# Two weight loads of a fused attention and GLU kernel issued from ScalarE's DMA queue

## The chip, the cores and the metric

The kernel runs on one core of a Trainium2 chip. The metric is the device time of one execution in microseconds (us); lower is better. All runs named here were fast, with a granted TensorE clock of 1.00 (0.999 in a few, 0.996 in one). The profile is of one execution, and its span is about 1.3 us shorter than the time of the same execution (557.7 against 558.93 for the kernel before).

## The reference, cut to what matters

```python
# x: (1, 2048, 576) bf16
xn = layernorm(x)
s  = attention(xn, wqkv, wo)          # 32 heads of 18, causal window of 256
g  = silu((sigmoid(xn @ w_gate) * (xn @ w_up)) @ w_down)   # w_gate, w_up: 576 x 4608
out = x + s * g
```

The first 512 rows of x are loaded and normalized, and then the gate/up products begin.

## The kernel before

The program is a graph of operations that a small scheduler puts into one list for each engine. The parts that matter:

```python
NWARM = (43, 10)      # warming products, two matmuls each
...
def load_x(self, c, i=0):             # the first four x tiles: four loads on SyncE
    if c == 0:
        for i in range(BPC):
            self.x_dma[i] = (self.dma(self.x0[:, i, :], self.x[i * P:(i + 1) * P, :], ...
...
zero = self.hT[:, 0, 0:P]
z = op("DVE", 920, lambda e: e.memset(zero, 0.0), "init:zero", prio=0)
...
self.op_tab = op("ACT", 1500, lambda e: e.activation(self.tring[:, 0, 0:1], zero[:, 0:1], ACTF.Exp), "init:tab",
                 deps=[z], prio=0)    # ScalarE's table load stands before it (0.79 to 2.07 us)
self.warm(NWARM[0], z, None, 107)     # TensorE multiplies zeros until x is there
...
def weights(wg):                      # one group: 256 columns of w_gate and of w_up, 256 KB each
    ds = [self.load_nat(self.wgs[:, sw, :, i, :], w[:, fc], f"dma:w:{c}:{wg}", ("w", sw, i), pr, [dw])
          for i, w in enumerate((self.wg, self.wu))]
    if wg % 2 == 0:                   # remainders: 64 rows for two groups, 64 KB each
        self.op_wgr[wg] = self.load_rem(self.wgr[:, sr, :], (self.wg[:, f8], self.wu[:, f8]), ...
...
def pair(eng, outs, lhs, rhs, start, stop, swap=0):   # every product: two matmuls on two row halves
    for i in range(2):
        t = i ^ swap
        res = eng.matmul(outs[i], lhs(ROWS[t], i), rhs(ROWS[t], i), start=start, stop=stop, tile_position=(64 * t, 0))
```

For each matmul TensorE has two instructions in its program, a weight load and the product (8342 of each in the profile); "instruction pair" below means these two. SyncE issues, in this order: four x tiles, the first group (gate, up), its two remainders, the second group, the second remainders, and so on.

The softmax here doesn't subtract the row's maximum and nothing guards it: scores larger than these inputs give would overflow.

Of the kernel before, what the change touches and what calls it, by code (L numbers as in the profile page):

```python
# [249 lines left out]
class Builder:  # L250
# [834 lines left out]
    def schedule(self):  # L1085
        ENGS = ("PE", "ACT", "DVE", "POOL", "SP")
        ops = self.ops
        remaining = [len(o.deps) + len(o.odeps) for o in ops]
        ready_t = [0.0] * len(ops)
        enabled = {e: [] for e in ENGS}  # L1090
        for i, o in enumerate(ops):
            assert o.cidx == i
            if remaining[i] == 0:
                enabled[o.eng].append(o)
        free = {e: 0.0 for e in ENGS}
        bw_clock = 0.0
        prog = {e: [] for e in ENGS}
        nsched = 0
        last_sc = 0.0
        while nsched < len(ops):  # L1100
            best = None
            for e in ENGS:
                cand = enabled[e]
                if not cand:
                    continue
                claims = {}
                if e == "PE":
                    for o in cand:
                        if o.acq is not None:
                            due = last_sc + o.space if o.space else 0.0  # L1110
                            claims.setdefault(o.acq.pool.name, []).append((o.prio, o.cidx, max(ready_t[o.cidx], due)))
                bk = None
                for o in cand:
                    st = max(free[e], ready_t[o.cidx])
                    early = 0.0
                    if o.space:
                        early = min(max(0.0, last_sc + o.space - st), FILL_NS)
                    units = None
                    if o.acq is not None:
                        mine = o.acq.pool  # L1120
                        barred = set()
                        for other in (self.pool_s, self.pool_f):
                            if other is not mine and any((p_, c_) < (o.prio, o.cidx) and r_ <= st + SHARE_NS
                                                         for p_, c_, r_ in claims.get(other.name, ())):
                                barred |= set(other.units)
                        got = mine.pick(o.acq.n, st, barred)
                        if got is None:
                            continue
                        st = max(st, got[0])
                        units = got[1]  # L1130
                        if any((p_, c_) < (o.prio, o.cidx) and r_ <= st + 300.0 for p_, c_, r_ in claims[mine.name]):
                            continue
                    k = (st + early + o.prio * self.PRIO_NS, o.cidx)
                    if bk is None or k < bk[0]:
                        bk = (k, o, st, units)
                if bk is not None and (best is None or (bk[2], ENGS.index(e)) < best[0]):
                    best = ((bk[2], ENGS.index(e)), bk)
            if best is None:
                left = [o.name for o in ops if o.idx < 0][:20]
                raise RuntimeError(f"scheduler stuck; unresolved ops e.g. {left}")  # L1140
            _, o, stt, units = best[1]
            if o.space:
                last_sc = stt
            if o.eng == "PE":
                if o.name.startswith("f1"):
                    for d in [d for d in ops if d.filler is not None and d.idx < 0]:
                        d.filler.rel.remove(d)
                        d.idx = nsched
                        nsched += 1
                        if d in enabled["PE"]:  # L1150
                            enabled["PE"].remove(d)
            enabled[o.eng].remove(o)
            if o.acq is not None:
                o.deps += [d for d in o.acq.pool.take(o.acq, units) if d not in o.deps]
            o.start = stt
            if o.lane is not None:
                free[o.eng] = stt + o.est
                o.end = max(stt + o.est + DMA_LAT_NS, bw_clock + o.nbytes / DMA_BYTES_PER_NS + DMA_QUEUE_NS)
                o.end += o.slack
                bw_clock = max(bw_clock, stt + o.est) + o.nbytes / DMA_BYTES_PER_NS  # L1160
            else:
                o.end = stt + o.est
                free[o.eng] = o.end
            o.idx = nsched
            nsched += 1
            prog[o.eng].append(o)
            for s_ in o.succs:
                remaining[s_.cidx] -= 1
                if s_.eng == o.eng:
                    lat = TURN_WAIT_NS if o.eng == "PE" and o in s_.deps else 0.0  # L1170
                elif o.lane is not None:
                    lat = DMA_PE_NS if s_.eng == "PE" else 90.0
                else:
                    lat = PE_OUT_NS if o.eng == "PE" else PE_IN_NS if s_.eng == "PE" else 50.0
                ready_t[s_.cidx] = max(ready_t[s_.cidx], o.end + lat)
                if remaining[s_.cidx] == 0 and s_.idx < 0:
                    enabled[s_.eng].append(s_)
        self.prog = prog
        if self.verbose:
            for e in ENGS:  # L1180
                busy = sum(o.est for o in prog[e] if o.filler is None)
                print(f"[sched] {e}: n={len(prog[e])} busy={busy / 1e3:.1f}us end={max(o.end for o in prog[e]) / 1e3:.1f}us")
# [97 lines left out]
```

## Time and profile before

| | before |
|---|---|
| median of 3 runs | 559.06 us (559.03 to 559.08) |
| span in the profile | 557.7 us |
| TensorE busy | 552.4 us (99%) |
| first gate/up product | 7.74 us |
| first x tile landed | 3.01 us |

The prediction shows the main lines. Two more turn out to matter, from the list of DMA queues on the page of the kernel before (packets, megabytes, share of the 16 DMA engines' time):

```profile
q1 hardware_dynamic: 105960, 60.68, 39.7%
...
q8 instruction: 66, 1.08, 0.8%
```

q1 is SyncE's queue. q8 brings instructions in 66 packets of 16 KB. TensorE's program has 8342 pairs and 221 other recorded instructions, 16,905 in all; 66 x 16,384 bytes over 16,905 is about 64 bytes for each, so this looks like TensorE's program streaming in, 256 instructions a packet. (The figure is rough: a part of the program was there before the first packet, which starts at 7.89 us, with TensorE at work from 1.05. The stops below give the 256 exactly.)

### The profile page before, as it was taken

What the parts mean: (1) busy time and instruction counts of PE and PEld (TensorE: products, weight loads), DVE (VectorE), ACT (ScalarE), POOL (GpSimd) and SP (SyncE); (2) the same over time, 40 slices, a digit from 0 to 9 for tenths busy, and PEclk for the clock granted to TensorE, in tenths of its full rate; (3) what the DMA queues carried; (4) which work ended last, traced back from release to release, by engine and by line L of the source; (5) the groups of instructions that cost most, each with busy time, mean ns of one, the idle gap of its engine ahead of it and who ended that gap; (6) DMA issues with size and microseconds to landing.
All of it is one profiled execution on the core that took longest, in us unless ns stands there. A gap on an engine that the chain in (4) does not pass through costs nothing.

```text
span 557.7 us, 19262 instructions
## 1 busy us (share of the span) xinstructions
PE 552.4 (99%) x8342; PEld 339.1 (61%) x8342; DVE 333.6 (60%) x797; ACT 274.3 (49%) x383; POOL 210.3 (38%) x360
## 2 busy tenths in 40 slices
PE   8999999999999999999999999999999999999997
PEld 7454444677755545457886555645588754444787
DVE  5477788787568667674558757357567623333133
ACT  4245654443656655645656464565756433223011
POOL 5564456566245454440667434034382200000000
PEclk9999999999999999999999999999999999999999
DMA  7988997831125535534121264234511035552010
GB/s 217 323 234 190 223 264 211 213 58 45 53 73 155 159 108 145 142 108 96 29 63 44 72 192 123 82 117 140 171 31 38 24 115 148 169 151 68 2 45 24
DMA packets 113468, 67.83 MB, mean 122 GB/s; under 512 B 18620, under 2 KB 111516, under 8 KB 113384
## 3 DMA queue, kind: packets, MB, share of 16 engines
q1 hardware_dynamic: 105960, 60.68, 39.7%
q0 software_dynamic: 7424, 5.92, 4.0%
q8 instruction: 66, 1.08, 0.8%
q14 instruction: 18, 0.15, 0.1%
HBM read 55.15 MB, written 2.36 MB: 103 GB/s over the span
## 4 chain that ended last, share of the span: by engine, by line
PE 98%; DVE 1%; DMA 0%; issue 0%; DVEq 0%
PE ps L122 95%; PE ps L801 3%; DMA x<-in_A_x_dram 0%; DVE small L525 0%; DVE small L527 0%; DVE xnr L541 0%; PE ps L599 0%; DVE s_attn L1062 0%; DVE thf L1067 0%; DVE xnr L545 0%; DVE small L529 0%; DVE small L531 0%; DVE xf L1072 0%; DVEq L1227 0%
## 5 line engine op out<-in xcount | busy, mean ns | idle before, releaser
L122 PE MATMUL ps<-xnT,wgs 64*128 64x512 bf16 (+1 forms) x2400 | 282.6, 368 | 0.2
L751 ACT ACTIVATE expr<-ps 128x1024 bf16<-128x1024 f32 (+4 forms) x160 | 154.9, 969 | 77.8 <-PE ps L122 77.2
L122 PEld LDWEIGHTS ps<-xnT,wgs 64*128 64x128 bf16 x2400 | 113.9, 94 | 115.0 <-DVE hT L949 1.6
L122 PE MATMUL ps<-wd_sb,hT 64*128 64x288 bf16 (+2 forms) x2448 | 156.7, 276 | 0.0
L949 DVE SCALAR_TENSOR_TENSOR hT<-tring,ps 128x512 bf16<-128x512 bf16 x144 | 98.3, 683 | 94.7 <-ACT tring L946 93.6
L946 ACT ACTIVATE tring<-ps 128x512 bf16<-128x512 f32 x144 | 86.1, 598 | 129.6 <-PE ps L122 127.5
L122 PEld LDWEIGHTS ps<-wd_sb,hT 64*128 64x128 bf16 x2448 | 112.5, 94 | 28.5
L279 POOL DMA_DIRECT2D qk<-qd x160 | 82.2, 521 | 119.9 <-PE ps L122 109.6
L764 DVE TENSOR_TENSOR expr<-expr,mask 128x128 bf16<-128x128 bf16 (+2 forms) x240 | 63.6, 299 | 62.3 <-ACT expr L751 61.7
L715 POOL TENSOR_SCALAR kx<-kprev,small 128x256 bf16<-128x256 bf16 x64 | 61.3, 967 | 28.2 <-PE ps L122 27.4
L122 PE MATMUL ps<-qk,kx 64*128 64x320 bf16 (+1 forms) x704 | 59.4, 254 | 0.0
L279 POOL DMA_DIRECT2D oT<-o2T x72 | 36.4, 513 | 58.7 <-DVE o2T L827 49.8
L122 PE MATMUL ps<-xnT,wgr 64*128 64x512 bf16 (+1 forms) x300 | 56.0, 367 | 0.0
L122 PEld LDWEIGHTS ps<-qk,kx 64*128 64x128 bf16 x704 | 31.2, 94 | 21.5 <-ACT expr L751 0.6
L122 PE MATMUL ps<-xnT,wqk 64*128 64x512 bf16 x256 | 32.6, 376 | 0.0
L1052 ACT ACTIVATE thf<-ps 128x576 bf16<-128x576 f32 (+3 forms) x22 | 11.4, 519 | 39.7 <-PE ps L122 39.4
L819 DVE STREAM_TRANSPOSE ot<-ps 128x512 f32<-128x512 f32 x32 | 22.4, 700 | 11.6 <-PE ps L801 11.5
L715 DVE TENSOR_SCALAR kx<-qk,small 128x512 bf16<-128x512 bf16 x64 | 22.4, 378 | 4.7 <-PE ps L122 4.1
L122 PEld LDWEIGHTS ps<-xnT,wgr 64*128 64x128 bf16 x300 | 14.9, 94 | 16.5
L827 DVE STREAM_TRANSPOSE o2T<-o 128x512 bf16<-128x512 bf16 x32 | 22.7, 711 | 1.0
L637 DVE CAST qd<-ps 128x1024 bf16<-128x1024 f32 (+1 forms) x20 | 22.1, 1111 | 1.5 <-PE ps L122 1.5
L697 ACT ACTIVATE v_aug<-ps 64x288 bf16<-64x288 f32 x32 | 13.1, 409 | 17.3 <-PE ps L122 16.8
(71 smaller groups left out, 300.9 us busy)
## 6 DMA issues: line engine op xcount, KB each, us to landing
wgs<-in_B_w_gate_dram SPq DMA_DIRECT2D x72, 256.0 KB, 3.3
wgs<-in_B_w_up_dram SPq DMA_DIRECT2D x72, 256.0 KB, 3.9
wd_sb<-in_B_w_down_dram SPq DMA_DIRECT2D x9, 576.0 KB, 6.3
qk<-qd POOLq DMA_DIRECT2D x100, 36.0 KB, 2.6
wgr<-in_B_w_gate_dram SPq DMA_DIRECT2D x36, 64.0 KB, 2.3
wgr<-in_B_w_up_dram SPq DMA_DIRECT2D x36, 64.0 KB, 2.7
xf<-in_A_x_dram SPq DMA_DIRECT2D x16, 144.0 KB, 2.6
out_dram<-xf SPq DMA_DIRECT2D x15, 144.0 KB, 1.8
```

The costliest lines, as they stand in the source:

```text
L122: res = eng.matmul(outs[i], lhs(ROWS[t], i), rhs(ROWS[t], i), start=start, stop=stop, tile_position=(64 * t, 0))
L279: o = self.op(eng, DMA_ISSUE_NS[eng], lambda e: e.dma_start(dst, src), name, deps, prio, nbytes=nbytes)
L637: return eng.tensor_copy(dst, self.both(h, n))
L697: return eng.activation(dst, src, ACTF.Copy)
L715: return e.tensor_scalar(self.kx[:, sx, pos:pos + n_ // SW, t, :], src.rearrange("p (s k) -> p s k", k=SW), self.half[:, t:t + 1], None, A ...
L751: return eng.activation(self.expr[:, se, :, lo * SW:NT], self.both(h, NT)[:, :, lo * SW:NT], ACTF.Exp, scale=SM_SCALE)
L764: return eng.tensor_tensor(e_, e_, m_, ALU.mult)
L801: res = eng.matmul(outs[i][p0:p0 + VH, cols], self.v_aug[ROWS[i], o:o + VH], self.expr[ROWS[i], se, t, cols], start=n == 0, stop=n == len( ...
L819: return e.transpose(self.ot1[:, p1, :], self.halves(hp, NT)[i])
L827: t2 = op("DVE", dve_ns(NT), lambda e, p2=p2, p3=p3: e.transpose(self.o2T[:, p3, :], self.o2[:, p2, :]), f"ot2:{c}:{pr}:{i}", deps=[on, d3 ...
L946: th = op("ACT", act_ns(NT), lambda e: e.activation(self.tring[:, st, :], bank(h, 0), ACTF.Tanh, scale=0.5), f"th:{c}:{ft}", deps=[pg, dt_ ...
L949: mu = op("DVE", dve_ns(NT), lambda e: e.scalar_tensor_tensor(self.hT[:, ft, :], self.tring[:, st, :], 1.0, bank(h, 1), ALU.add, ALU.mult) ...
```

## The change

The intent: start the first weight loads while SyncE is still busy with x, on a queue that is idle then, and let SyncE go on 1 us sooner with what follows. ScalarE issues the two loads right after the dummy activation (2.09 to 2.30 us in the trace of the kernel before) that follows its table load (0.79 to 2.07).

```diff
@@ at the end of the scheduler
+        first = [o for o in prog["SP"] if o.name == "dma:w:0:0"]
+        for o in first:
+            prog["SP"].remove(o)
+            o.eng = "ACT"
+            o.deps.append(self.op_tab)
+        at = prog["ACT"].index(self.op_tab) + 1
+        prog["ACT"][at:at] = first
         self.prog = prog
```

Nothing else in the five programs changes.

## The prediction

> **What bounds the kernel now.** I read the page's busy shares first, then a table of engine busy time by stretch, then the chain of waits, and last the timeline of the first ten microseconds. The shares and the table say where there is anything to win:
>
> ```profile
> PE 552.4 (99%) x8342; PEld 339.1 (61%) x8342; DVE 333.6 (60%) x797; ACT 274.3 (49%) x383; POOL 210.3 (38%) x360
> ...
> 0.00:7.70 7.70, 5.68 (x126) 5.22 (x126) 4.38 (x17) 3.74 (x8) 2.97 (x12) 1.00 0.72 197
> 7.70:12.20 4.50, 4.46 (x156) 4.24 (x158) 2.10 (x15) 1.39 (x2) 2.82 (x4) 1.00 0.87 249
> 12.20:554.60 542.40, 542.25 (x8068) 329.61 (x8061) 325.88 (x762) 268.68 (x372) 204.47 (x345) 1.00 0.44 120
> ```
>
> The first figure after the comma is TensorE's busy time. From 12.2 to 554.6 us TensorE is idle 0.15 us (542.40 less 542.25). The whole body is TensorE's own work at full clock, so a load that comes earlier there is worth nothing. A change in the loading order can act only through the moment at which TensorE starts its first real product; from then on, a shift of that moment is a shift of the end. The chain of waits shows that moment:
>
> ```profile
> 0.80 2.21 DMA x<-in_A_x_dram
> ...
> 6.66 0.41 DVE xnr L541
> 7.06 0.02 issue
> 7.09 0.19 DVE xnr L545
> 7.28 0.04 issue
> 7.32 0.32 PE ps L599 x10
> 7.64 0.10 issue
> 7.74 1.00 PE ps L122 x26
> ```
>
> The first x tile lands at 3.01 us. VectorE does the layer norm of two tiles until 7.28, TensorE transposes the second tile (L599) from 7.32, and the gate/up stream (L122) begins at 7.74. The reader is to distrust the "0.10 issue" before it: that is time for which the profile found no wait. The timeline of what is concerned shows more:
>
> ```profile
> 2.09 0.21 ACT L452 ACTIVATE tring<-hT 128x1 bf16<-128x1 bf16 x1
> ...
> 2.66 0.43 SPq L279 DMA_DIRECT2D wgs<-in_B_w_gate_dram  x1
> 3.14 0.51 SPq L279 DMA_DIRECT2D wgs<-in_B_w_up_dram  x1
> 3.69 0.55 SPq L279 DMA_DIRECT2D wgr<-in_B_w_gate_dram  x1
> 4.28 0.59 SPq L279 DMA_DIRECT2D wgr<-in_B_w_up_dram  x1
> ...
> 4.48 0.68 ACT L586 ACTIVATE tring<-x 128x576 bf16<-128x576 bf16 x1 [2.19 <-DMA x<-in_A_x_dram]
> ...
> 7.71 0.80 PEld L122 LDWEIGHTS ps<-xnT,wgs 64*128 64x128 bf16 x24 [0.19 <-issue]
> ```
>
> By the list of DMA issues in a narrow window, the gate load of 2.66 lands 4.1 us later (6.76) and the up load of 3.14 lands 4.5 us later (7.64). The first weight load of the stream is at 7.71, 0.07 us after that. So two paths end almost together: the norm of the second tile, and the landing of the up weights; the landing is the later one. Without it the stream would follow the transposes as it does later in the same timeline, where transposes at 8.56 and 10.03 are followed by products at 8.71 and 10.17, 0.14 to 0.15 us later. That would be 7.32 + 0.15 = 7.47, so the landing holds TensorE for 7.74 - 7.47 = 0.27 us.
>
> The trace also has the landing of each of the 16 increments of a load. Those of the up load come at 6.06 to 6.54 for thirteen of them, and at 6.91, 7.37 and 7.60 for three: the wait is for the slowest of the 16 DMA engines.
>
> [...]
>
> **The change part by part.** (1) *Removed from SyncE:* two issues, 2.66 to 3.69, so 1.03 us. The small gate/up remainders (wgr) are issued at about 2.66 in place of 3.69, and everything behind them up to 1.03 us earlier. Worth nothing directly: TensorE waits for none of it (the remainder's last share is in at 8.16, first used at 8.45 by the weight loads).
>
> (2) *Added to ScalarE:* two issues after the dummy activation that ends at 2.09 + 0.21 = 2.30. At SyncE's 0.43 and 0.51 us they occupy 2.35 to about 3.35. ScalarE's next work is at 4.48 and waits for the third x tile, so about 1.1 us of its 2.19 us idle time is left. Cost 0[...].
>
> (3) *Moved in time:* the gate issue from 2.66 to 2.35, the up issue from 3.14 to about 2.85: 0.3 us earlier each. SyncE's first load is issued at 0.80 and its first packet moves at 1.84, so 1.04 us: the gate data can flow from 3.4.
>
> (4) *Moved in order:* before, one row serves x, then the gate and up weights, then the remainders, then the second group. x packets (1152 B) run from 1.84 to 4.53, weight packets (512 B) from 3.96. After, the weights have a row to themselves[...]. At 3.4 about 350 KB of x had moved and 226 KB were left, 14 KB per engine; the first group is 512 KB, 32 KB per engine. [...] Two live rows may also move more than one: with 64 and 144 KB loads beside each other at 14 to 16 us the core moved 348 GB/s, against 256 to 280 at 2 to 4 us. [...] The stragglers' lag of about a microsecond comes on top in both cases. [...] I put the landing 0.2 to 0.9 later than 7.64, mid 0.5.
>
> (5) *x tiles delayed by the sharing:* the fourth lands at about 4.84, used at 5.85, and may come 0.3 to 0.6 later: hidden. The third (4.46) may come 0.1 to 0.3 later; its statistics feed the norm at 7.49 and the transposes at 8.56, where the copy ended at 8.14: 0.4 us of room.
>
> (6) *Given back:* while the stream starts late, the other waits fill. The four groups of 24 products take 0.95, 0.87, 1.03 and 0.86 us; the two long ones carry about 0.1 and 0.2 of hidden waits. I give back 0.15. Sum: 0.5 - 0.15 = +0.35 us.
>
> **The rivals.** *The weights come first:* the load is issued 0.3 us sooner and its row gets served at once, so it lands before 7.47. For it: the issue gap is real, and the wait at 7.64 is on the path. But the norm of the second tile takes its place: at most 0.27 us, and the fourth transposes at 10.03 need a copy that ends at 9.75, which leaves 0.25. It would be 558.8 us. *The sharing at its worst:* [...]+1.2 us: 560.2. Against it is the higher rate seen with more loads in flight. *The third x tile becomes the bound:* at +0.5 us its chain (ScalarE 4.48, GpSimd, VectorE 7.49) delays the third transposes by 0.1: 559.2; it would hide under a late start. *Nothing moves:* the same total of bytes, the same stragglers, landing within 0.1 of 7.64: 559.0.
>
> **Range and chances.** Predicted 559.06 + 0.35 = 559.4 us. The low end is the first rival, 558.75; the high end just under the worst sharing, 560.1. Two per cent is 11.2 us; TensorE's idle time before the stream is 7.70 - 5.68 = 2.0 us in all, so faster by that much can't be, and slower would need a start 11 us late. Chances: faster 0.003, same 0.992, slower 0.005.
>
> **What would show it right or wrong.** ScalarE's queue with two issues from about 2.35 and SyncE's remainder issues at about 2.7 show (1) to (3). If (4) is right, x packets run on past 4.53, the first stream product comes at 8.0 to 8.5 in place of 7.74, and the end shifts by as much less 0.15. If it comes at 7.5, the first rival is right and the weights weren't slowed by sharing. Wrong altogether I would be if the body from 12.2 gained or lost idle time, or the granted clock changed.

The forecast's sum came to 0.5 - 0.15 = +0.35 us on 559.06. The working of the 0.5 and what the +1.2 us of the worst rival was made of took for granted how two queues share the DMA engines, which no run here shows. So take 0.5 and 1.2 as assumptions. A "row" is one DMA queue as the page lists it, like q1.

## The result

The changed kernel's median was 559.84 us (559.55 to 560.22, 4 runs) against 559.04 (558.83 to 559.08, 4 runs). The ratio was 1.0015, with a 95% interval of 0.9998 to 1.0033: the same at the 2% scale, and some 0.9 us slower if one looks closely. All ratios here are the mean time of one kernel's fast runs over that of the other's fast runs of the same rounds, so not quite the ratio of the medians quoted.

The profile after is of the slowest of its runs (560.22 us; span 558.9 against 557.7). First the busy shares and the stretches of the same table as before:

```profile
PE 552.9 (99%) x8342; PEld 339.8 (61%) x8342; DVE 333.8 (60%) x797; ACT 274.2 (49%) x383; POOL 210.0 (38%) x360
```

```profile
0.00:7.70 7.70, 5.81 (x128) 5.43 (x129) 4.21 (x16) 3.72 (x7) 2.65 (x12) 1.00 0.81 201
7.70:12.20 4.50, 3.61 (x119) 3.02 (x118) 2.30 (x15) 1.41 (x2) 2.58 (x5) 1.00 1.18 287
12.20:554.60 542.40, 542.26 (x8068) 330.35 (x8063) 324.95 (x760) 268.38 (x372) 204.77 (x345) 1.00 0.44 120
```

The body has not changed (542.26 us busy, before 542.25). All of the loss lies between 7.70 and 12.20, where TensorE is busy 3.61 us in place of 4.46. The chain of waits after shows where:

```profile
1.71 3.30 DMA x<-in_A_x_dram
...
7.41 0.32 PE ps L599 x10
7.73 0.96 PE ps L122 x26
8.69 0.31 PE ps L599 x10
9.00 1.30 PE ps L122 x46
10.31 0.31 PE ps L599 x10
10.61 0.11 PE ps L122 x3
10.72 0.89 issue
11.61 12.79 PE ps L122 x166
```

The stream begins at 7.7 as before. Then, at 10.72, stands 0.89 us of "issue": the profile knows of nothing that TensorE waited for. The timelines of TensorE before and after, at this place:

```profile
10.03 0.31 PE L599 MATMUL ps<-ident,xnr 64*128 64x64 bf16 x10
10.17 1.03 PE L122 MATMUL ps<-xnT,wgs 64*128 64x128 bf16 x24
```

```profile
10.29 0.32 PE L599 MATMUL ps<-ident,xnr 64*128 64x64 bf16 x10
10.45 0.27 PE L122 MATMUL ps<-xnT,wgs 64*128 64x128 bf16 x3
11.61 0.80 PE L122 MATMUL ps<-xnT,wgs 64*128 64x128 bf16 x21 [0.89 <-issue]
```

The stop comes after 3 matmuls of a half turn of 8, which the program issues without a wait inside it. TensorE's sequencer has no semaphore event in the trace between 9.86 and 12.51. So it is not a wait for data. In the single records of the trace, the 221st weight load is at 10.45 and the 222nd at 11.61 (1.15 us, rounded from the records). And the kernel before has the same hole at the same weight load: 10.18 to 10.40, 0.22 us. The group of 24 that took 1.03 us in place of 0.86 was hiding it.

ScalarE's timeline after (start, duration, what), and from the page after the line of the new DMA queue:

```profile
2.32 0.43 ACTq L279 DMA_DIRECT2D wgs<-in_B_w_gate_dram  x1
2.79 0.52 ACTq L279 DMA_DIRECT2D wgs<-in_B_w_up_dram  x1
...
5.03 0.68 ACT L586 ACTIVATE tring<-x 128x576 bf16<-128x576 bf16 x1 [2.74 <-DMA x<-in_A_x_dram]
```

```profile
q10 hardware_dynamic: 1056, 0.52, 0.3%
```

q10 is the new row, with the two loads of 256 KB. Their issue went as predicted. The third x tile came later (ScalarE starts on it at 5.03 in place of 4.48). And in the trace's record of every DMA packet, the first 16 KB packet of the instruction queue ran from 7.89 to 9.01 before, and from 8.99 to 10.25 after. TensorE went on 1.39 us after the packet's end before (10.40), and 1.36 us after it in the changed kernel (11.61).

Lined up weight load by weight load, the changed kernel is 0.05 us ahead at the start of the stream, 0.27 us behind after the fourth transposes (the late third tile), 1.20 us behind after the 222nd weight load, and 1.2 us behind at the end. Nothing is gained or lost after that.

### The profile page after: what moved, and what is told of

The parts are those of the page before. It is cut to its first block, busy times and chain, and to the rows that moved or that the text cites. A ratio compares the mean times of both kernels' runs of the same rounds, so it can differ in the third digit from the quotient of the medians.

```text
span 558.9 us, 19261 instructions
## 1 busy us (share of the span) xinstructions
PE 552.9 (99%) x8342; PEld 339.8 (61%) x8342; DVE 333.8 (60%) x797; ACT 274.2 (49%) x383; POOL 210.0 (38%) x360
## 4 chain that ended last, share of the span: by engine, by line
PE 98%; DMA 1%; DVE 0%; issue 0%; SPq 0%; ACT 0%; POOL 0%; DVEq 0%
PE ps L122 94%; PE ps L801 3%; DMA x<-in_A_x_dram 1%; PE ps L599 0%; SPq L279 0%; ACT tring L586 0%; DVE s_attn L1062 0%; POOL small L533 0%; DVE xnr L541 0%; DVE thf L1067 0%; DVE xf L1072 0%; POOL small L587 0%; DVE xnr L545 0%; DVEq L1234 0%
```

## The experiments

**Theory A:** TensorE runs out of instructions. The packet that holds the next ones is late, because the loads issued 1 us sooner stand before it in the DMA engines. **Theory B:** a late load of x or of weights stops TensorE, and the profile fails to name it. All "stops" below are read from the single weight-load records of the profiled run. In every kernel I compare the mean time with that of the kernel before in the same rounds.

### The changed kernel again

No edit.

> The changed kernel once more, to see what is constant in it. In its first profile TensorE stood from 10.45 to 11.61 us in the middle of a turn (after 3 of 8 products, with no semaphore event between 9.86 and 12.51). Theory A (instruction fetch): the stop is at the 221st weight load of TensorE in every run, and its length follows the 16 KB packet of the instruction queue (before: 7.89 to 9.01, stop 0.22 us; changed: 8.99 to 10.25, stop 1.16 us), so TensorE resumes 1.3 to 1.4 us after that packet ends; the time is 559.5 to 560.3, spread by the length of the stop. Theory B (a late load of x or weights is what stops it): the stop moves about from run to run with the landings, and is not tied to the packet.

Median 560.47 us (559.63 to 560.82, 5 runs) against 559.31 (558.62 to 559.57, 9 runs): ratio 1.0017, interval 1.0003 to 1.0030, so 1.0 us slower, now clear of noise. The stop is at the same weight load, 10.19 to 11.93, 1.75 us. The packet ran from 9.42 to 10.64; TensorE went on 1.29 us after its end. Its timeline:

```profile
10.18 0.27 PE L122 MATMUL ps<-xnT,wgs 64*128 64x128 bf16 x3
11.94 0.80 PE L122 MATMUL ps<-xnT,wgs 64*128 64x128 bf16 x21 [1.48 <-issue]
```

The place is fixed; the length varies with the packet, and so does the time. As A has it.

### More instructions in the warming, before and after

```diff
-NWARM = (43, 10)
+NWARM = (17, 50, 10)      # 34 matmuls of 128 columns, 100 of 64: 48 pairs more
-        self.warm(NWARM[0], z, None, 107)
+        self.warm(NWARM[0], z, None, 107); self.warm(NWARM[1], z, self.warm_last, ..., 64)
```

> The kernel before, with its 86 warming products (128 columns) made into 34 of 128 and 100 of 64 columns: 48 more TensorE instruction pairs in about the same time, nothing else changed, no load moved. Theory A: the hidden stop of 0.22 us moves 48 pairs earlier in the work (still at the 221st weight load, now in the second tile's products near 9.1 us), the fetch is asked for earlier, near 6 us, and the stop gets shorter or goes: 558.8 to 559.0, at best 0.2 us less than before. Theory B: the gap stays at the same product of the work (third tile, fourth product), 559.0.

> The changed kernel with the same 48 more instruction pairs in the warming. Theory A: the stop of 1.16 us is no longer at the third tile's fourth product; it is at the 221st weight load and down to 0 to 0.4 us, as the fetch is asked for about 1.5 us earlier: 558.9 to 559.3, so 0.5 to 1.0 us less than the changed kernel of the same rounds. What stays is the third x tile's delay (0.26 us at the fourth transposes). Theory B: as the changed kernel, 559.5 to 560.2.

Times: 560.23 us median for the padded kernel before (ratio 1.0020, interval 1.0007 to 1.0032), 559.82 for the padded changed one (1.0009, 0.9997 to 1.0022). The gap at the third tile's fourth matmul went in both. That alone doesn't rule out B, since both kernels now lose time before that place; the kernels with fewer instructions, below, do. My times were wrong, and so was the guess of where the stop would be. The packet now came at 6.00 to 6.99 and at 6.22 to 7.42, and the block boundary was passed without a stop. Two new losses took its place in each (0.74 and 1.15 us between weight loads in the kernel before, 1.16 and 1.13 in the changed one). TensorE's timeline of the padded kernel before:

```profile
8.49 0.40 PE L122 MATMUL ps<-xnT,wgs 64*128 64x128 bf16 x8 [0.50 <-DMA wgr<-in_B_w_up_dram]
...
13.33 0.38 PE L122 MATMUL ps<-xnT,wgs 64*128 64x512 bf16 x2
14.44 0.82 PE L122 MATMUL ps<-xnT,wgs 64*128 64x512 bf16 x6 [0.73 <-issue]
```

At 8.49 TensorE waited for one share of the up remainder: 14 of its 16 shares were in by 7.53, the last at 8.40. The packet of 16 KB took 0.99 us (the first two packets of each run took 0.95 to 1.37, save one of 1.55). I infer that it held one DMA engine for that time, and that the late share was this engine's; the trace doesn't name the engine. The changed kernel shows the same more plainly: in each of the five loads issued from 5.63 us on, one share lands 1.2 to 1.3 us after the other fifteen, and in the load issued before them, at 5.07, only 0.26 us after; its packet took 1.26 us. At 13.33 comes the next stop, after 348 pairs, 1.40 us after the end of the second packet (12.09 to 13.04). Counted in recorded instructions, two for each pair plus the others of TensorE: the stop of the kernel before is after 2 x 221 + 7 = 449, this one after 2 x 348 + 9 = 705. 705 - 449 = 256, one packet to the instruction.

### Fewer instructions in the warming

```diff
-NWARM = (43, 10)
+NWARM = (11, 5)           # 22 matmuls of 512 columns, 10 of 256: 74 pairs fewer
-        zero = self.hT[:, 0, 0:P]
+        zero = self.hT[:, 0, 0:NT]
```

> The kernel before with 74 fewer TensorE instruction pairs in the warming (22 products of 512 columns and 10 of 256 in place of 86 and 20 of 128, about the same time). Theory A: the instruction packet is asked for 74 pairs later in the work (starts near 10 to 10.5 us, when the first weight group and its remainders have landed by 8.4), the 221st weight load is now in the 512-column part near 13 us, where a pair takes 0.2 us, so the stop goes: 0 in place of 0.2 to 0.4 us and no share of the first group is late: 0.2 to 0.4 us under before. Theory B (not the instruction supply): the gap stays after 3 of 8 products of the third tile, same time as before.

> The changed kernel with the same 74 fewer pairs. Theory A: the stop of 1.2 to 1.7 us goes, and what stays of the change is the third x tile's delay, 0 to 0.3 us: 0.8 to 1.2 us under the changed kernel (559.8 to 560.5), so 0.0 to 0.3 us over before_fewer of the same rounds. If the change has another cost that the stop only covers, it shows here: over 0.5 us above before_fewer. Theory B: as the changed kernel.

Medians 560.50 us and 560.56, ratios 1.0023 (1.0010 to 1.0035) and 1.0023 (1.0011 to 1.0036): a clear miss. I had expected the stop to vanish; it moved 73 pairs later in the work, and grew. TensorE's timeline of the kernel before with fewer pairs:

```profile
12.22 1.19 PE L122 MATMUL ps<-xnT,wgs 64*128 64x512 bf16 x14
14.75 0.23 PE L122 MATMUL ps<-xnT,wgs 64*128 64x128 bf16 x2 [1.33 <-issue]
```

It stops after 220 pairs and 9 others: 449 recorded instructions again. The packet ran from 12.19 to 13.34, 2 us later than I had thought, and TensorE went on 1.41 us after it. The stop moved with the count of instructions alone, with no load moved; that settles the kind of the stop for A. In these two kernels the stop is alike (1.60 and 1.56 us), and so are the mean times, 560.23 and 560.27. So no cost of the change beside the stop is seen here, though five runs of each, spread over 1.4 to 2.0 us, would not show a small one.

### SyncE held back, ScalarE still issuing

```diff
+        next(o for o in prog["SP"] if o.name == "dma:wgr:0:0").deps.append(self.x_dma[1][0])
```

> The changed kernel, with SyncE's first remainder load made to wait for the second x tile (lands at 3.47), so that SyncE goes on at about 3.5 in place of 2.66, nearly as before (3.69). ScalarE still issues the two weight loads. If SyncE's head start of 1 us (more queued on each DMA engine when the instruction fetch comes) makes the fetch late: packet back near 8 us, stop 0.2 to 0.4 us, 559.0 to 559.3. If a second queue row as such makes it late: packet near 9, stop about 1 us, 559.5 to 560.2. The x tiles: the third still lands late (near 5.0) if the weights on ScalarE's row delay it.

Median 559.15 us (558.78 to 560.04), ratio 1.0001 (0.9989 to 1.0014): the change without SyncE's head start shows no loss (the changed kernel lost 1.0 us in the same rounds). SyncE went on at 3.39, the packet came at 8.41 to 9.64, the stop was 0.50 us (TensorE's timeline):

```profile
10.44 0.28 PE L122 MATMUL ps<-xnT,wgs 64*128 64x128 bf16 x3
10.95 0.80 PE L122 MATMUL ps<-xnT,wgs 64*128 64x128 bf16 x21 [0.23 <-issue]
```

Five runs can't resolve less than some 0.7 us, but the trace says the same: with the two loads still on ScalarE's queue, most of the stop is gone with SyncE's head start.

> The changed kernel with SyncE held to the second x tile's landing and 74 fewer pairs: whether the two mends add up. Theory A: no stop to mend is left, so holding SyncE adds nothing: within 0.2 us of after_fewer. The first stream product comes at 7.5 to 8.0, set by the slowest share of the up weights.

The same hold with 74 pairs fewer: median 559.32 us (1.0009, 0.9995 to 1.0023), mean 0.9 us under the changed kernel with fewer pairs. My "within 0.2 us" missed, because it supposed that no stop was left there. The packet came at 10.91 in place of 12.15, and the stop was 0.34 us in place of 1.56.

### Half of the change

```diff
-        first = [o for o in prog["SP"] if o.name == "dma:w:0:0"]
+        first = [o for o in prog["SP"] if o.name == "dma:w:0:0"][:1]
```

> Half of the change: only the gate load goes to ScalarE's queue, the up load stays on SyncE, whose head start is then 0.5 us in place of 1.03. Theory A with the head start as the reason of the late packet: it starts between that of before (7.89) and of the changed kernel (8.99, 9.42), near 8.4 to 8.7, and the stop at the 221st weight load is 0.5 to 0.9 us: 559.3 to 559.8. If any second row makes it late: stop over 1.1 us, 559.8 to 560.5.

Median 559.49 us (559.21 to 559.84), mean 0.54 us over before in the same rounds (ratio 1.0010, 0.9997 to 1.0022). The packet ran from 8.31 to 9.57, the stop was 0.76 us. Half the head start, about half the loss.

### Which loads stand before the packet

The first form of A held that the packet waits for whatever is queued when TensorE nears its last instructions, at about 7.5 us. The next two kernels keep all but hold SyncE later, at the second remainders, until the second tile's transposes end.

```diff
+        next(o for o in prog["SP"] if o.name == "dma:wgr:0:2").deps.append(next(o for o in prog["PE"] if o.name == "tr:1"))
```

> The changed kernel, in which SyncE holds the remainders of the second weight pair (and all behind them) until TensorE has ended the second tile's transposes (7.6 us in place of 5.07). They are first used near 20 us. This keeps SyncE's head start for the first loads but empties the queues by the time of the instruction packet. Theory A with the queue's backlog as the reason of the late packet: it starts at 7.6 to 8.2 (changed kernel 8.99 and 9.42), the stop at the 221st weight load is 0 to 0.3 us, and the time is 558.7 to 559.3. If the two queue rows as such were the reason, the packet starts near 9 again: 559.8 to 560.5. If the held loads come too late for later work, a new wait shows after 12 us.

> The kernel before with the same hold (second remainders from 6.09 to 7.6 us). Theory A: the packet starts at 7.5 to 7.9 (7.89), the stop of 0.22 us shrinks to 0 to 0.2: 558.7 to 559.0, so 0 to 0.3 under before. A new wait after 12 us if the held loads are late.

Both missed. In the changed kernel the packet still ran late, 8.80 to 9.84, and the stop was 1.12 us (TensorE's timeline):

```profile
10.07 0.28 PE L122 MATMUL ps<-xnT,wgs 64*128 64x128 bf16 x3
11.20 0.80 PE L122 MATMUL ps<-xnT,wgs 64*128 64x128 bf16 x21 [0.85 <-issue]
```

The median was 559.64 us, 0.5 over before in the mean (1.0010, 0.9997 to 1.0022). In the kernel before it came at 7.88, where it came without the hold (7.89); the median was 559.14 us (1.0003, 0.9989 to 1.0017). The stop there didn't shrink but grew to 0.65 us: the packet took 1.37 us in place of 1.12, and TensorE was 0.19 us sooner at this place. A second wait, of 0.36 us from 15.06, is for the last share of the held third group (15.31). So the loads issued from 5.07 on in the changed kernel, and from 6.09 on in the kernel before, hardly set when the packet starts. In the changed kernel with the hold (run after_late) the packet starts at 8.80, just as the last packets of the second weight group end (8.80). Laid beside the issue times of all runs, a simple order appears: the packet starts behind the loads that had been issued by about 5 us, and before the later ones.

| kernel | second group issued (gate, up) | packet | stop |
|---|---|---|---|
| before | 4.91, 5.54 | 7.89 to 9.01, between the two | 0.22 |
| changed | 3.89, 4.51 | 8.99 to 10.25, behind both | 1.15 |
| changed, again | 3.89, 4.52 | 9.42 to 10.64, behind both | 1.75 |
| SyncE held | 4.62, 5.25 | 8.41 to 9.64, between | 0.50 |
| gate only | 4.35, 4.99 | 8.31 to 9.57, behind both | 0.76 |
| changed, later loads held | 3.89, 4.52 | 8.80 to 9.84, behind both | 1.12 |
| before, later loads held | 4.89, 5.52 | 7.88 to 9.25, between | 0.65 |

"Between" and "behind both" are read from the shares: from the first load that comes after the packet on what I infer to be its engine, one share more than before is late (by 1.2 to 1.3 us in the padded changed kernel). In the kernel before, with SyncE held and with the later loads held, this starts with the second up load (issued at 5.25 to 5.54); in the others with a later load. So loads issued at 4.99 and 5.07 are still in front of the packet, and one issued at 5.25 is not. The head start of 1.03 us brings the second up load and the next gate remainder, 320 KB more, in front of the packet, which starts about 1 us later (7.89 against 8.99). The place in the line doesn't set the start alone: with the gate load only, the same second group is in front, and the packet starts at 8.31. The 16 shares of one load are not equally far along (6.06 to 7.60 us for the first up load of the kernel before), and the packet, I infer, stands behind one of them; which one, the trace doesn't show.

The record allows one step more. Count 256 recorded instructions back from the stop, to the point where 193 (in some kernels 194) have run. TensorE is there at 5.66 to 5.88 us in the nine profiled runs with the old warming, at 4.46 in the two padded ones, and at 8.93 to 9.21 in the three with fewer pairs. The first packet moves with it: 6.79 to 9.42, 6.00 and 6.22, 10.91 to 12.19. So the packet seems to be asked for at about the time when TensorE starts on the last 256 instructions that it has, and comes 1.0 to 3.6 us later, behind the loads issued before. That is why changing the warming only moved the stop, and why 5 us, and not 7.5, is the time that counts. The trace doesn't show the request, so this is inferred from the times.

That order can be tested: hold the second group itself.

```diff
+        next(o for o in prog["SP"] if o.name == "dma:w:0:1").deps.append(next(o for o in prog["PE"] if o.name == "tr:1"))
```

> The changed kernel with the hold already at the second weight group (issued at 7.7 in place of 3.89). Then nothing shares the DMA engines with ScalarE's two loads after the first remainders: the up weights land at 6.8 to 7.1 in place of 7.4 to 7.6, the stream begins at 7.45 to 7.55 as the norm of the second tile allows, and the packet starts at once (7.5 to 7.7), no stop. The second group is used near 12 us and must land by then: with 512 KB from 7.7 it lands at 10.5 to 11.5. 558.5 to 558.9, the fastest of all; if the second group lands after 12, a new wait takes it back: 559 to 560.

TensorE's timeline, at the old place of the stop and later:

```profile
10.50 0.85 PE L122 MATMUL ps<-xnT,wgs 64*128 64x128 bf16 x24
...
16.19 1.90 PE L122 MATMUL ps<-xnT,wgs 64*128 64x512 bf16 x16 [0.63 <-DVE hT L949]
```

The packet now ran from 6.79 to 8.12, just behind the first group, and the stop is gone: 24 matmuls in one piece. The median was 559.05 us (1.0002, 0.9988 to 1.0015). The gain was handed back: held this long, the third group lands at 16.05, and TensorE would have gone on at about 15.4 (14.53 and four pairs of 0.216 us; the line names VectorE, which had ended long before; the last share of the third up load lands 0.14 us ahead of the start). I had taken the third group to be needed near 20 us, which was wrong.

### A version to beat both

The kernel before, nothing on ScalarE, the second group held only until the first tile's transposes end:

```diff
+        next(o for o in prog["SP"] if o.name == "dma:w:0:1").deps.append(next(o for o in prog["PE"] if o.name == "tr:0"))
```

> The kernel before, no load on ScalarE's queue, with SyncE holding the second weight group until TensorE has ended the first tile's transposes (issue at about 6.0 us in place of 4.91). In all runs so far the instruction packet takes its place behind the loads that were issued before about 5 us: after the first half of the second group in the kernel before, after all of it in the changed kernel, and after the first group alone where the second was held to 7.7. If that is so, here it stands behind the first group and its remainders alone: it starts at 6.6 to 7.2 and ends by 8.4, and the stop of 0.22 us at the 221st weight load goes. The second group lands by 10.5 (used at 12), the third by 14.3 (used at 14.8). 558.6 to 558.9, 0.1 to 0.3 under before: the fastest. If the place in the queue is not what counts, the packet starts at 7.5 or later, and the time is as before; if the third group is late, a wait near 14.8 takes the gain back.

Median 558.81 us (558.53 to 559.58, 5 runs) against 559.00 (558.88 to 559.95, 9 runs): ratio 0.9995, interval 0.9981 to 1.0008. The packet ran from 7.18 to 8.14 and the stop is gone from TensorE's timeline:

```profile
10.30 0.85 PE L122 MATMUL ps<-xnT,wgs 64*128 64x128 bf16 x24
```

The profiled run was the slowest of the five (559.58). Its chain of waits shows what can still happen:

```profile
9.88 5.80 DMA wgs<-in_B_w_up_dram
15.68 0.14 issue
```

There one share of the third up load came at 15.68 with 14 of the 16 in by 13.23. The second instruction packet ran from 13.39 to 14.34 in that time; whether it held up this share isn't shown. The median is 0.2 us under that of the kernel before in the same rounds, but the interval spans 1, so that it is faster is not shown.

## Why the prediction was right or wrong

The number held: 559.4 was predicted with 558.75 to 560.1, and 559.84 came. The second set, on a chip where the kernel before had 559.31, gave 560.47, over the upper end, and a difference of 1.0 us in the mean where 0.35 had been predicted. So the number was right by luck: the sum came out near for reasons that were largely not those given. Point by point:

- **Where a gain or loss can come from.** Right: the body kept 542.26 us, and what happened before 12.2 us went through to the end unchanged (1.20 us behind at the 224th weight load, 1.2 at the end).
- **(1) SyncE's head start.** The time was right (remainder issue at 2.66). "Worth nothing directly" was the step that failed: it was the costly part. With it held back, no loss was left to see (1.0001).
- **(2) ScalarE's issues.** Right: 2.32 and 2.79, 0.43 and 0.52 us, not stretched by SyncE's beside them (which took 0.55 and 0.59, as before), and done 1.7 us before ScalarE's next work.
- **(3) Earlier data.** Wrong in size: the row's first packet moved at 4.19 (3.77 in the repeat), not 3.4. Before, the first weight packet had moved at 3.96, so an issue 0.34 us sooner brought the data no sooner in the profiled run.
- **(4) The weights slowed by sharing.** Half right. x packets ran on to 5.05 as far as the records of SyncE's row go (4.53 before), and the middle shares of the up load landed at 7.06 in place of 6.47, 0.6 later, near the 0.5 forecast. How the two rows share the engines is not shown; from 4.75 to 6.25 us the packet records have 0.41 MB in ScalarE's row and 0.09 MB in SyncE's. But "the stragglers' lag of about a microsecond comes on top in both cases" failed: the last share came at 7.55 in place of 7.60, the spread between middle and last being 0.5 us in place of 1.1. The rival "nothing moves" was right for the landing: the term of +0.5 us measured -0.05. One reading in this part was also wrong. The 348 GB/s at 14 to 16 us was taken for two rows with loads of 64 and 144 KB; the trace has all packets of that stretch in SyncE's one row, and the loads in flight were of 576, 256 and 72 KB. That two rows move more was therefore not supported by it. In the changed kernel the core did move more with both rows live, 295 GB/s from 4 to 7.8 us against 261 before.
- **(5) The third x tile.** Right in kind, too small in size: it landed 0.55 us later (5.01 against 4.46), not 0.1 to 0.3 (0.28 in the repeat, 4.74), and showed as 0.27 us at the fourth transposes. In the profiled run the stop for instructions came after it.
- **(6) Given back.** The prediction saw the long group of 1.03 us and called what it hid "about 0.1 and 0.2 of hidden waits" that would fill. It was the stop for instructions, and it grew to 1.15 us. To ask what that wait was for, with no semaphore in it, would have led to the cause.

The cause, as shown: a stop tied to the 449th recorded instruction (or the 705th), in every kernel that has one, that ends 1.24 to 1.51 us after the end of the 16 KB packet (12 stops); and a packet that moves with the loads issued before about 5 us. When TensorE asks for the packet is an inference from the order of landings and the count of instructions; the trace doesn't show the request.

## What to carry to other kernels

TensorE's program, as it looks, came in during the run, in 66 packets, and the first of them started at 8.99 us in place of 7.89 with 320 KB more of loads issued by about 5 us. A burst of prefetched loads early in a kernel, where instructions are short and used up fast (256 in 4.4 us in the kernel before, from 5.79 to 10.18), can leave an engine without instructions: the stop grew from 0.22 to 1.15 us here. Look for a stop inside a stretch that has no wait, named "issue", at the same instruction count in every run, and set it beside the packets of the instruction queue. Issuing loads sooner was not free here, though nothing seemed to wait (1.0 us in the repeat): what is needed last should not stand in the line ahead of what is needed first.
